# Score and maximum products of an attention layer, each split over the four 32-column tiles of TensorE

## The chip, the cores and the metric

The kernel runs on one core of one Trainium2 chip. The metric is the device time of the whole program in microseconds. A core has a matrix engine (TensorE, PE in the profile, with its weight loads shown apart as PEld), a vector engine (DVE), an activation engine (ACT), a general engine (POOL) and a queue engine (SP) that issues most of the transfers. PE writes to PSUM, which has eight banks of 128 partitions by 512 float32 here divided into three pools.

## The reference, cut to what matters

Two layers of the same shape, each an attention block and a small routed feed-forward block; only the attention matters here. S = 2048 tokens, D = 512, H = 32 query heads of 16 columns each, one key and one value head for all of them.

```python
q = (x @ wq).reshape(B, S, H, Dh)            # 32 heads of 16
k = x @ wk                                   # one key head
v = x @ wv                                   # one value head
scores = einsum("bhqd,bkd->bhqk", q, k) * (Dh ** -0.5)
p = softmax(scores, axis=-1)
o = einsum("bhqk,bkd->bhqd", p, v)
x = x + o.reshape(B, S, H * Dh) @ wo
```

Everything is float32 in and out.

## The kernel before, in words

**Units and steps.** A layer has 32 units (`u`), each of four heads by 512 query tokens, and a unit has 16 steps (`t`), so `layer` runs 512 steps. Each step makes four *scores* (128 keys by 512 columns of queries) and four *maximum products* (128 queries by 512 keys).

**Two products of the same operands.** `max_mm` multiplies 128 query columns by 512 keys into a bank of the pool psM (tile `pM`, four banks), and `nc.vector.reduce_max` (line 431) takes the row maximum of the bank into `mx`. This runs ahead of the scores by up to 12 steps. `scores` multiplies 128 keys by 512 query columns into a bank of the pool psS (tile `pS`, three banks), with the negated maximum in two extra rows, and ACT takes the exponential from PSUM (line 483) into `pr`. Both products are float16 and hold 48 or 50 rows of contraction: the operands `q_st` and `k_st` stand at partitions 0 to 49 and at 64 to 113, for two different pairs of heads. `h` picks the half; `max_mm` takes half `1 - n % 2` where the score beside it takes half `i % 2`, so a score and the maximum product next to it stand on different halves of the rows.

**The float32 products.** `pv_mm` multiplies `pr` by the values into the bank `pO` (line 510). It is issued as four products of 128 rows by 32 columns, one for each group of 32 PSUM partitions. `by_columns` (lines 184 to 188) does the same for the projections that `between` fits into free parts of that bank, and for others. A float32 product stands in the trace as two rows.

**What sets the order.** The program is in the order in which Python calls it (`manual_schedule`): per step `scores`, `max_mm` four times in turn, and after every third score (`RUN` = 3) a batch of `pv_mm` and one `between` piece. Below, a *score phase* is the three scores and three maximum products between two such batches, an *O phase* is the batch of 128-row products between two score phases, and a *round* is one of each. Other steps (projections, normalization, stores) are hung on steps by number.

Of the kernel before, what the change touches and what calls it, by code (L numbers as in the profile page):

```python
# [17 lines left out]
P = 128  # L18
# [6 lines left out]
CW = S // NCH  # L25
# [30 lines left out]
def interleaved_layers(ctx, tc, x_in, wq, wkv, wo, w_r, w_gate, w_up, w_down, out):  # L56
    nc = tc.nc
# [126 lines left out]
    def by_columns(out, lhsT, rhs, start, stop, shared=False):  # L184

        for j in range(4):
            r = slice(32 * j, 32 * (j + 1))
            nc.tensor.matmul(out[r], lhsT[:, r], rhs, start=start, stop=stop, skip_group_check=shared)  # L188
# [16 lines left out]
    def bank():  # L205
        pm = psM.tile([P, CW], F32, name="pM")
        return pm
# [102 lines left out]
    q_st, parts, pqs = {}, {}, {}  # L310
# [76 lines left out]
    def layer(li, src_d, dst_d, early=None):  # L387
        xld = xl_d[li]
        k_st, v_ext = k_sts[li], v_exts[li]
# [26 lines left out]
        def max_mm(mi, n):  # L416
            u, i = divmod(mi, 16)
            if i == 0 and n == 0:
                mx[u] = work.tile([P, 4, 16], F32, name="mx", bufs=3)
            pm = bank()  # L420
            nq = cuts[u]

            b, r = divmod(i, 16 // nq)
            x, c = divmod(r, 2)
            j, s = divmod(x, 4 // nq)
            h, c = 1 - n % 2, 2 * c + n // 2
            q = (b * 4 // nq + s) * P
            r = slice(h * HR, h * HR + KQ)
            nc.tensor.matmul(pm, q_st[u][r, j, q:q + P], k_st[r, c * CW:(c + 1) * CW], start=True, stop=True)  # L429
            i = b * 16 // nq + h * 8 // nq + 2 * s + j  # L430
            nc.vector.reduce_max(mx[u][:, c, i:i + 1], pm, axis=AX.X)  # L431

# [32 lines left out]
        def scores(t, i):  # L465

            u, r = divmod(t, KT)
            nq = cuts[u]
            b, r = divmod(r, KT // nq)
            w = CW // nq  # L470
            nk = nq // 2

            ps = bank() if mi == 16 * NU and i % 2 else psS.tile([P, CW], F32, name="pS")
            i, h = divmod(i, 2)
            hs = 2 * t + i
            if h == 0:
                pr[hs] = work.tile([P, 2, CW], F32, name="pr", bufs=6)
            rows = slice(h * HR, h * HR + KM)
            for k in range(nk):
                kt = r * nq + i * nk + k  # L480
                nc.tensor.matmul(ps[:, k * 2 * w:(k + 1) * 2 * w], k_st[rows, kt * P:(kt + 1) * P],  # L481
                                 q_st[u][rows, :, b * w:(b + 1) * w], start=True, stop=True)
            nc.scalar.activation(pr[hs][:, h, :], ps, AF.Exp, scale=DH ** -0.5)  # L483

        def pv_mm(hs, halves):
# [313 lines left out]
        for p in range(NCH * NG):  # L799
            e = 32 * p  # L800
            if p + 1 < NCH * NG:
                for n in range(4):
                    w = slice(n * P, (n + 1) * P)
# [10 lines left out]
            c, g = divmod(p - 1, NG)  # L814
            u = 2 * p - 1
# [7 lines left out]
        for c in range(NCH):  # L823
# [13 lines left out]
            for n, (t, kind) in enumerate(when):  # L837
                i = c * TPC + n // 4
                w = slice(n % 4 * OW, (n % 4 + 1) * OW)
# [98 lines left out]
        w = slice(2 * P, CW)  # L938
# [22 lines left out]
        for t in range(-LEAD0, last):  # L961
            tiles = []
            while mi < 16 * NU and made(mi) <= t:
                tiles.append(mi)
                mi += 1
            mms = [(m, n) for m in tiles for n in range(4)]
            mms = [first[4 * m + n] if 4 * m + n < len(first) else (m, n) for m, n in mms]
            for i in range(4):
                if t >= 0:
                    scores(t, i)  # L970
                for m, n in mms[len(mms) * i // 4:len(mms) * (i + 1) // 4]:
                    max_mm(m, n)
                if i == 3:
                    held.append(t)
                n = 4 * t + i
                if t < 0 or n % RUN == RUN - 1:

                    done = False
                    left = (n - RUN + 1) // 2 * 2 - ready
                    left = min(left, HALVES + (left > HALVES + 1))  # L980
                    while left > 0 and not done:
                        halves = range(ready % 2, 2) if left > 1 else range(ready % 2, ready % 2 + 1)
                        done = pv_mm(ready // 2, halves)
                        ready += len(halves)
                        left -= len(halves)
                    if ready and not done:
                        between(*at_block[0])
                    while held:
                        run(held.pop(0))
# [76 lines left out]
        for k in range(NDC):  # L1066
            for j in range(4):
                nc.tensor.matmul(gate[32 * j:32 * (j + 1), :FC], xsT[:, k, :], wgate_sb[:, k, j * FC:(j + 1) * FC],
                                 start=k == 0, stop=k == NDC - 1)
# [81 lines left out]
        for h in range(2):  # L1151
            w = slice(h * dh, (h + 1) * dh)
            for k in range(4):
                for j in range(4):
                    nc.tensor.matmul(pd[h][32 * j:32 * j + 2, :dh], hT[:, k, j, :], wd[4 * j + k][:, w],
                                     start=k == 0, stop=k == 3)
# [3 lines left out]
        for h in range(2):  # L1160
            w = slice(h * dh, (h + 1) * dh)
# [25 lines left out]
        for k in range(NDC):  # L1187
            if k % 2 == 0:
                w = slice(k * P, (k + 2) * P)
# [16 lines left out]
        w = slice(0, P)  # L1206
# [5 lines left out]
        for h in range(2):  # L1212
            r = slice(h * HR, h * HR + KQ)
# [5 lines left out]
        w = slice(P, 2 * P)  # L1219
# [38 lines left out]
    w = slice(0, 2 * P)  # L1258
# [61 lines left out]
```

## Time and profile before

| | |
|---|---|
| median of 2 runs | 2690.03 us (2689.11 to 2690.96) |
| the profiled execution | 2689.6 us |
| its span, first to last instruction | 2687.5 us |
| mean granted clock of TensorE | 0.986 of 2.4 GHz |
| PE, DVE, ACT busy | 2634.3, 2573.5, 2280.4 us |

Busy time of PE is the time in which at least one product is in the array by the trace's modelled ends. Products overlap, so its share doesn't say how much room PE has. That of DVE and ACT is the time in which an instruction of theirs runs.

### The profile page before, as it was taken

The numbers are of one execution on the slowest core, as the hardware profiler recorded it, in microseconds if no ns is written. First come the engines' busy times: TensorE is split into PE (matmuls) and PEld (weight loads), VectorE is DVE, ScalarE is ACT, GpSimd is POOL, SyncE is SP. The second block draws the span as 40 slices with busy tenths as digits, with TensorE's granted clock in tenths as the row PEclk, the third lists the DMA queues.
The fourth block names the chain that finished last, engine by engine and source line by source line (L and its number), as shares of the span: only waits on it lengthen the run. The fifth ranks groups of instructions, "written<-read, shape, count | busy, mean of one in ns | idle before, by whom it ended". The sixth has DMA issues, their size and how long they took to land.

```text
span 2687.5 us, 94488 instructions
## 1 busy us (share of the span) xinstructions
PE 2634.3 (98%) x39780; PEld 1238.4 (46%) x39780; DVE 2573.5 (96%) x4499; ACT 2280.4 (85%) x4710; POOL 770.1 (29%) x2039
## 2 busy tenths in 40 slices
PE   7999999999999999999999999999999999999999
PEld 3544444444444444444555444444444444444445
DVE  8999999999999999999669999999999999999995
ACT  2888888988889898889718888889898898988895
POOL 2100001122462126625521010021224522164262
PEclk8999999999999999999969999999999999999999
DMA  3001110000110001011400000000001100010114
GB/s 99 6 26 29 32 58 11 13 12 15 38 38 15 11 13 47 29 31 35 140 15 6 15 15 13 29 11 15 9 15 38 39 12 11 23 36 27 31 49 131
DMA packets 70764, 83.11 MB, mean 31 GB/s; under 512 B 27740, under 2 KB 43676, under 8 KB 70340
## 3 DMA queue, kind: packets, MB, share of 16 engines
q1 hardware_dynamic: 67474, 75.80, 9.2%
q8 instruction: 313, 5.13, 0.8%
q10 hardware_dynamic: 2354, 1.07, 0.1%
q14 instruction: 111, 0.91, 0.1%
q0 software_dynamic: 512, 0.20, 0.0%
HBM read 42.80 MB, written 17.18 MB: 22 GB/s over the span
## 4 chain that ended last, share of the span: by engine, by line
PE 78%; ACT 10%; DVE 5%; DMA 2%; issue 2%; POOL 2%; SPq 1%; ACTq 0%; DVEq 0%; POOLq 0%
PE pO L510 33%; PE pS L481 23%; PE pM L429 11%; ACT pr L483 8%; PE pO L188 5%; DVE mx L431 5%; PE pS L188 2%; DMA q_st<-mr 1%; SPq L460 1%; PE pM L454 1%; ACT so L516 1%; ACT qf L640 1%; DMA x<-xl_d,of 1%; ACT xT L259 0%; PE pS L258 0%
## 5 line engine op out<-in xcount | busy, mean ns | idle before, releaser
L431 DVE TENSOR_REDUCE mx<-pM 128x1 f32<-128x512 f32 x4096 | 2474.2, 683 | 30.6 <-PE pM L429 28.2
L483 ACT ACTIVATE pr<-pS 128x512 f32<-128x512 f32 x4044 | 2124.7, 605 | 237.4 <-PE pM L429 199.5
L429 PE MATMUL pM<-k_st,q_st 48*128 48x512 f16 x4096 | 1224.4, 385 | 8.8 <-DVE mx L431 5.8
L481 PE MATMUL pS<-q_st,k_st 50*128 50x512 f16 (+1 forms) x4248 | 1168.5, 371 | 17.4 <-DMA q_st<-mr 3.5
L510 PE MATMUL pO<-pr,v_ext 128*32 128x128 f32 (+1 forms) x22528 | 1174.9, 328 | 5.4 <-ACT so L516 3.2
L510 PEld LDWEIGHTS pO<-pr,v_ext 128*32 128x32 f32 x22528 | 562.3, 109 | 666.3 <-issue 453.5
L481 PEld LDWEIGHTS <-k_st 50*128 50x128 f16 x4352 | 298.2, 95 | 495.5 <-issue 350.6
L429 PEld LDWEIGHTS <-q_st 48*128 48x128 f16 x4096 | 288.7, 94 | 131.7 <-issue 101.9
L445 POOL TENSOR_SCALAR ma<-ma 128x8 f32<-128x8 f32 (+1 forms) x136 | 32.2, 237 | 809.1 <-DVE ma L439 809.1
L641 POOL TENSOR_TENSOR x<-x,qf 128x128 f32<-128x128 f32 x128 | 58.1, 455 | 493.6 <-ACT qf L640 493.5
L188 PE MATMUL pO<-xT,wq_sb 128*32 128x128 f32 x3584 | 180.0, 273 | 0.0
L346 POOL CAST qh<-qf 128x128 f16<-128x128 f32 x120 | 34.8, 290 | 444.2 <-ACT qf L345 434.6
L188 PE MATMUL pO<-wo_sb,so 128*32 128x128 f32 x2816 | 137.0, 273 | 0.0
L188 PEld LDWEIGHTS pO<-xT,wq_sb 128*32 128x32 f32 x3584 | 111.3, 110 | 34.0
L662 POOL TENSOR_TENSOR xh<-xh 128x128 f32<-128x128 f32 (+7 forms) x384 | 97.9, 255 | 30.1
L188 PEld LDWEIGHTS pO<-wo_sb,so 128*32 128x32 f32 x2816 | 86.6, 110 | 24.0
L724 POOL TENSOR_TENSOR xh<-xh 128x256 f32<-128x256 f32 (+8 forms) x216 | 66.4, 308 | 15.0
L516 ACT COPY so<-pO 128x256 f32<-128x256 f32 (+1 forms) x136 | 52.6, 387 | 2.1 <-PE pO L510 2.1
L456 ACT CAST mr<-pM 16x128 f16<-16x128 f32 (+1 forms) x136 | 34.6, 254 | 23.3 <-PE pM L454 14.6
L347 POOL TENSOR_TENSOR ql<-qf,qh 128x128 f16<-128x128 f32 x120 | 51.4, 428 | 9.7
L708 POOL TENSOR_SCALAR xh<-x,mv,rs 128x512 f32<-128x512 f32 x24 | 50.0, 2083 | 0.0
L188 PE MATMUL pS<-wo_sb,so 128*32 128x128 f32 (+1 forms) x896 | 41.9, 319 | 0.0
(260 smaller groups left out, 986.0 us busy)
## 6 DMA issues: line engine op xcount, KB each, us to landing
q_st<-mr SPq DMA_DIRECT2D x512, 1.0 KB
q_st<-qh SPq DMA_DIRECT2D x244, 32.0 KB
zt<-zr_d SPq DMA_DIRECT2D x120, 64.0 KB
xl_d<-xh SPq DMA_DIRECT2D x28, 256.0 KB
pr<-in_w_up SPq DMA_DIRECT2D x12, 448.0 KB
x<-in_x SPq DMA_DIRECT2D x20, 256.0 KB
x_d<-x SPq DMA_DIRECT2D x16, 256.0 KB
x<-x_d SPq DMA_DIRECT2D x16, 256.0 KB
```

The lines of the kernel that those rows point to most:

```text
L188: nc.tensor.matmul(out[r], lhsT[:, r], rhs, start=start, stop=stop, skip_group_check=shared)
L347: nc.gpsimd.tensor_tensor(ql, qf, qh, op=OP.subtract)
L429: nc.tensor.matmul(pm, q_st[u][r, j, q:q + P], k_st[r, c * CW:(c + 1) * CW], start=True, stop=True)
L431: nc.vector.reduce_max(mx[u][:, c, i:i + 1], pm, axis=AX.X)
L481: nc.tensor.matmul(ps[:, k * 2 * w:(k + 1) * 2 * w], k_st[rows, kt * P:(kt + 1) * P], q_st[u][rows, :, b * w:(b + 1) * w], start=True, sto ...
L483: nc.scalar.activation(pr[hs][:, h, :], ps, AF.Exp, scale=DH ** -0.5)
L510: nc.tensor.matmul(po[u][32 * j:32 * (j + 1), b * w + q.start:b * w + q.stop], v_ext[:, kt, 1 - u % 2:33 - u % 2], p[:, j % 2, k, j // 2, ...
L516: nc.scalar.copy(so[u][:, b * w:(b + 1) * w], po[u][:, b * w:(b + 1) * w])
L641: nc.gpsimd.tensor_tensor(x1[i][:, w], x1[i][:, w], y, op=OP.add)
L662: g.tensor_tensor(t[:, :n], t[:, :n], t[:, n:2 * n], op=OP.add)
L708: eng.tensor_scalar(xl, x1[i], mv2[m][:, b, 0:1], rs2[m][:, b:b + 1], op0=OP.subtract, op1=OP.mult)
L724: nc.gpsimd.tensor_tensor(rp_t[i][:, :n], rp_t[i][:, :n], rp_t[i][:, n:2 * n], op=OP.add)
```

## The change

Both float16 products go through `by_columns`, which the kernel already has: one product of 64 rows by 128 columns becomes four of 64 rows by 32 columns, each with its own weight load, on the column tiles j = 0 to 3, and each writes 32 partitions of the same bank. The moving operand, 512 elements long (256 where a unit is cut in four), is the same for the four. Nothing else is changed.

```diff
--- before.py
+++ after.py
@@ max_mm @@
             r = slice(h * HR, h * HR + KQ)
-            nc.tensor.matmul(pm, q_st[u][r, j, q:q + P], k_st[r, c * CW:(c + 1) * CW], start=True, stop=True)
+            by_columns(pm, q_st[u][r, j, q:q + P], k_st[r, c * CW:(c + 1) * CW], True, True)
             i = b * 16 // nq + h * 8 // nq + 2 * s + j
             nc.vector.reduce_max(mx[u][:, c, i:i + 1], pm, axis=AX.X)
@@ scores @@
-                nc.tensor.matmul(ps[:, k * 2 * w:(k + 1) * 2 * w], k_st[rows, kt * P:(kt + 1) * P],
-                                 q_st[u][rows, :, b * w:(b + 1) * w], start=True, stop=True)
+                by_columns(ps[:, k * 2 * w:(k + 1) * 2 * w], k_st[rows, kt * P:(kt + 1) * P],
+                           q_st[u][rows, :, b * w:(b + 1) * w], True, True)
```

PE's queue in the first layer before the change, the end of an O phase and the first two scores and maxima of the score phase behind it. What a product waits for stands in brackets, `Activation` for a free bank of psS and `DVE` for one of psM.

```order
L510 MATMUL pO<-pr,v_ext_117 32x128 x4
L188 MATMUL pO<-xT,wq_sb 32x128 x4
L481 LDWEIGHTS k_st
L481 MATMUL pS<-q_st,k_st 128x512 [waits Activation_49]
L429 LDWEIGHTS q_st
L429 MATMUL pM<-k_st,q_st 128x512 [waits DVE_49]
L481 LDWEIGHTS k_st
L481 MATMUL pS<-q_st,k_st 128x512 [waits Activation_49]
L429 LDWEIGHTS q_st
L429 MATMUL pM<-k_st,q_st 128x512 [waits DVE_49]
```

PE's queue after the change, the last of the four products of a score, the four of the maximum product next to it, and the O phase behind them. The two float16 products now carry the line of the helper, 188.

```order
L188 LDWEIGHTS k_st
L188 MATMUL pS<-q_st,k_st 32x512
L188 LDWEIGHTS q_st
L188 MATMUL pM<-k_st,q_st 32x512 [waits DVE_49]
L188 LDWEIGHTS q_st
L188 MATMUL pM<-k_st,q_st 32x512
L188 LDWEIGHTS q_st
L188 MATMUL pM<-k_st,q_st 32x512
L188 LDWEIGHTS q_st
L188 MATMUL pM<-k_st,q_st 32x512
L510 MATMUL pO<-pr,v_ext_117 32x256 x4
L510 MATMUL pO<-pr,v_ext_117 32x128 x4
```

A score phase thus grows from 6 loads and 6 products to 24 and 24, in the same order of scores and maxima, with each wait on the first of its four products. The queues of the other engines stand as before.

## Rows read from the trace of the kernel before

**Rows 1.** The page: the span, the engines' busy time, DVE's busy tenths in 40 slices, and the chain that ended last.

```profile
span 2687.5 us, 94488 instructions
...
PE 2634.3 (98%) x39780; PEld 1238.4 (46%) x39780; DVE 2573.5 (96%) x4499; ACT 2280.4 (85%) x4710; POOL 770.1 (29%) x2039
...
DVE  8999999999999999999669999999999999999995
...
PE 78%; ACT 10%; DVE 5%; DMA 2%; issue 2%; POOL 2%; SPq 1%; ACTq 0%; DVEq 0%; POOLq 0%
```

**Rows 2.** Groups of instructions by line and shape over the whole span: busy us, mean ns of one, idle time of the engine before them and what ended it.

```profile
L431 DVE TENSOR_REDUCE mx<-pM 128x1 f32<-128x512 f32 x4096 | 2474.2, 683 | 30.6 <-PE pM L429 28.2
L483 ACT ACTIVATE pr<-pS 128x512 f32<-128x512 f32 x4044 | 2124.7, 605 | 237.4 <-PE pM L429 199.5 <-PE pS L481 16.6 <-PE pM L481 8.5
L429 PE MATMUL pM<-k_st,q_st 48*128 48x512 f16 x4096 | 1224.4, 385 | 8.8 <-DVE mx L431 5.8 <-DMA q_st<-qh 1.6 <-ACT mr L456 0.5
...
L510 PEld LDWEIGHTS pO<-pr,v_ext 128*32 128x32 f32 x22528 | 562.3, 109 | 666.3 <-issue 453.5 <-ACT so L516 50.8 <-ACT qf L345 19.3
L481 PEld LDWEIGHTS <-k_st 50*128 50x128 f16 x4352 | 298.2, 95 | 495.5 <-issue 350.6 <-DMA q_st<-mr 5.0
```

**Rows 3.** The waits of DVE from 60 to 2640 us, longest first: who waited for whom, us in total, times, longest us.

```profile
DVE mx L431 <- PE pM L429: 26.7, 63, 1.6
DVE qf L607 <- PE pM L600: 7.3, 4, 3.6
```

**Rows 4.** PE's timeline (start us, us, instruction, count) around two rounds near 1080 us, where PE has no pause, and before them one long stretch of 128x32 products. Rows of the same kind that follow each other are merged, the length reaching to the end of the last.

```profile
1076.87 1.06 PE L188 MATMUL pS<-wo_sb,so 128*32 128x128 f32 x32
...
1079.69 0.28 PE L454 MATMUL pM<-ident,mp 128*16 128x128 f32 x1
1079.90 0.39 PE L481 MATMUL pS<-q_st,k_st 50*128 50x512 f16 x1
1079.90 0.60 PE L429 MATMUL pM<-k_st,q_st 48*128 48x512 f16 x2
1080.13 0.59 PE L481 MATMUL pS<-q_st,k_st 50*128 50x512 f16 x2
1080.35 0.38 PE L429 MATMUL pM<-k_st,q_st 48*128 48x512 f16 x1
1080.66 0.86 PE L510 MATMUL pO<-pr,v_ext 128*32 128x256 f32 x16
1081.33 0.40 PE L188 MATMUL pO<-wo_sb,so 128*32 128x128 f32 x8
1081.66 0.39 PE L481 MATMUL pS<-q_st,k_st 50*128 50x512 f16 x1
```

**Rows 5.** The same view near 703 us, a score phase in which PE waits, and the two reductions of DVE before it.

```profile
702.52 0.39 PE L481 MATMUL pS<-q_st,k_st 50*128 50x512 f16 x1
702.53 0.39 PE L429 MATMUL pM<-k_st,q_st 48*128 48x512 f16 x1
702.75 0.38 PE L481 MATMUL pS<-q_st,k_st 50*128 50x512 f16 x1
703.02 0.40 PE L429 MATMUL pM<-k_st,q_st 48*128 48x512 f16 x2
703.23 0.38 PE L481 MATMUL pS<-q_st,k_st 50*128 50x512 f16 x1
703.54 0.86 PE L510 MATMUL pO<-pr,v_ext 128*32 128x256 f32 x16
...
701.68 1.28 DVE L431 TENSOR_REDUCE mx<-pM 128x1 f32<-128x512 f32 x2
```

**Rows 6.** PE's groups by line and shape from 2100 to 2400 us.

```profile
L429 PE MATMUL pM<-k_st,q_st 48*128 48x512 f16 x492 | 144.6, 381 | 0.0
L481 PE MATMUL pS<-q_st,k_st 50*128 50x512 f16 x492 | 140.5, 380 | 1.9 <-DMA q_st<-mr 0.4
L510 PE MATMUL pO<-pr,v_ext 128*32 128x256 f32 x1312 | 101.9, 385 | 0.4
L510 PE MATMUL pO<-pr,v_ext 128*32 128x128 f32 x1312 | 67.9, 279 | 0.0
L188 PE MATMUL pO<-xT,wq_sb 128*32 128x128 f32 x488 | 24.5, 273 | 0.0
L188 PE MATMUL pO<-wo_sb,so 128*32 128x128 f32 x428 | 20.8, 273 | 0.0
L454 PE MATMUL pM<-ident,mp 128*16 128x128 f32 x16 | 4.4, 277 | 0.0
L188 PE MATMUL pS<-wo_sb,so 128*32 128x128 f32 x64 | 2.1, 274 | 0.0
```

**Rows 7.** Busy us (and instructions) of PE, PEld, DVE, ACT and POOL in three stretches, then the granted clock, the DMA share and GB/s.

```profile
701.52:701.55 0.03, 0.03 (x6) 0.02 (x4) 0.03 (x1) 0.03 (x1) 0.03 (x1) 1.00 0.00 0
...
2100.00:2400.00 300.00, 297.68 (x4604) 136.54 (x4604) 298.21 (x512) 268.98 (x554) 95.90 (x249) 1.00 0.07 22
78.00:98.00 20.00, 20.00 (x475) 14.39 (x475) 19.36 (x35) 16.71 (x36) 3.64 (x14) 1.00 0.01 3
```

**Rows 8.** The weight loads near the end of the program (line 1127), where products of 46 rows by 2 columns are followed by ones of 128 rows by 2 columns.

```profile
2678.89 0.08 PEld L1127 LDWEIGHTS pM<-token,hot 46*2 46x2 f32 x2
...
2679.01 0.11 PEld L1127 LDWEIGHTS pM<-token,hot 128*2 128x2 f32 x3
```

## The prediction

> **What bounds the kernel now.** The page comes first [rows 1]. PE is busy 98% of the span and its own chain blames PE for 78%, but both rest on modelled ends of products that overlap; neither says that PE is short of time. DVE is busy 2573.5 of 2687.5 us, and its tenths are nines except at the change of layer and the ends. The groups say with what [rows 2]: 4096 reductions of a maximum bank take 2474.2 us, 604 ns of DVE each, and in all of them DVE idled 30.6 us. In a stretch of full stream, 2100 to 2400 us, DVE is busy 298.2 of 300 us [rows 7]. The reductions are the bound, and the change touches none of them. Their part in PE's hands is the wait for a maximum product, 26.7 us in 63 places between 60 and 2640 us [rows 3]; the rest of DVE's idle time lies in the layer change, the start and the tail, which hold next to no score products. So a faster PE can give at most some 27 us, 1.0%. What a slower PE costs depends on its room.
>
> That room is seen in two timelines. Near 1080 us PE has no pause [rows 4]: score and maximum product start together at 1079.90, the second pair 0.23 us later, the third at 1080.35, the O phase at 1080.66. A pair takes 0.22 us as one product would, so the two halves of the rows run at the same time, and the unhindered score phase takes 0.76 us. In the second pair the maximum product stands in the record no later than the score that precedes it in the queue, so PE lets a row half that is free go first. Near 703 us [rows 5] the second maximum product waits until 703.02, just behind the reduction that ended at 701.68 + 1.28 = 702.96: its bank was not free. That score phase takes 1.02 us, because PE waits for DVE.
>
> Round by round, from 2100 to 2400 us [rows 6]: 492 scores are 164 rounds of 1.829 us. The groups of four 128x32 products take 0.109 us at 128 columns (eight groups in 1076.87 to 1077.93, seven steps and a last product of 0.27 to 0.28 us [rows 4]), and I take 0.218 at 256. There are 1312/4 = 328 groups of 256 and (1312 + 488 + 428 + 64)/4 = 573 of 128: 71.5 + 62.5 = 134 us, 0.82 us a round. The way back from the O phase costs 0.10 us on top (last group of 128 near 1081.44, next score 1081.66, 0.11 expected), the first group after a switch some 0.02, and the transposes (16 of 0.2 us in 164 rounds) 0.02. PE needs 0.76 + 0.82 + 0.14 = 1.72 us of 1.83 us. Its room is about **0.11 us a round**, with rounds of 16 products in the O phase far below and rounds of 24 (1.76 us from 1079.90 to 1081.66) close to the three reductions, 3 x 0.604 = 1.81 us.
>
> **The change, part by part.** All of it lies in the score phase, whose unhindered length I call 0.76 + X; the whole question is X against 0.11.
>
> *Issue.* A pair has eight loads and eight products instead of two and two. Between 701.52 and 701.55 four loads and four products of 128x32 start [rows 7]: 7 ns for a load and its product where the column tiles differ. Eight pairs of load and product are thus 0.055 us of issue in a pair's 0.22 us, and it doesn't add up from pair to pair, as groups of four follow each other at 0.109 us, the pace of one. What is left is skew: the maximum product's four start after the score's four, 4 x 7 = 28 ns later rather than 3, and the fourth column 3 x 7 = 21 ns behind the first. The last product of the phase starts about 0.045 us later, less what the pairs now lose to each other: **X = +0.035 us**.
>
> *Streaming.* Four moving streams of 64 rows in each half replace one. No row shows float16 on column tiles. The bounds are the pair in one pass (0.22 us, X as above) and no overlap of the halves or half-speed streams (0.44 us a pair, X = 0.66). I take the first: the 128x32 float32 products are four streams at once and lose nothing to each other [rows 4].
>
> *Switching.* From the last pair (1080.35) to the O phase (1080.66) pass 0.31 us, 0.09 more than a pair, and 0.10 on the way back. The new tile has the columns of the O phase's tile but not its rows. The nearest row is at the end of the program [rows 8]: the load of 128 rows by 2 columns starts 0.12 us after the pair of loads of 46 rows by 2 columns, where loads of one shape start within 0.03 us. So a change of rows alone still costs about 0.09, and I count no gain; the bounds are 0 and -0.19 us a round.
>
> *Weight loads.* They lie behind the running products but for the first after a switch; the row of the old load is 95 ns for 128 columns of float16, that of a 32-column load in float32 109 ns [rows 2]. At worst +0.015 us a round, inside the room. The Trainium skill speaks against the change here: TensorEngine Tiling (Array Packing), Restrictions and Gotchas, says that column tiling excludes Fast Weight Load. The two rows agree with it in so far as a quarter of the columns takes no less time; by it the sum would move by those 0.015 us at most, some 2 us in the end.
>
> *On the other engines* nothing changes. A maximum product's bank is full 0.05 us later; the four banks cover 4 x 0.6 = 2.4 us, so DVE doesn't see that. A score is ready as much later; ACT idles 237 us before its exponentials [rows 2].
>
> *The sum.* X = 0.035 leaves a mean room of 0.075 us. It costs where the room is already gone: behind the 63 waits of DVE. Counting two to three rounds for each (what four banks can bridge), 63 x 2.5 x 0.035 = 5.5 us. Against the profiled execution's 2689.6 us (0.4 below the median of 2690.03, which changes nothing) that gives **2695 us**. The skill's TensorE: Matmul & The Clock Gate, Measured speedup vs the span model, has about 4 ns for each further tile where this trace shows 7; by it X would be 0.02 and the sum 2693.
>
> **The rivals.**
>
> *A, a faster switch.* If the same column width spares the drain, the round loses 0.19 us and PE's waits on DVE grow instead. DVE's 26.7 us are all there is to win: about 2668 us. For it: both switches are visible gaps. Against it: rows 8. Chance 0.08.
>
> *B, strict order.* With 24 loads and 24 products in the phase PE may not look past a blocked row half as it does now. Then each pair waits for the one before in queue order, 28 ns at each of three and the skew: X about 0.09, mean room 0.02. The room spreads by some 0.11 to either side (O phases of 16 and of 24 products differ by 0.22 us), over three rounds some 0.06, so a mean shortfall of 0.015 us in 1365 rounds: +20 us, 2712 us. Chance 0.13.
>
> *C, the streams don't overlap* (slower). A score phase of six products in a row, 6 x 0.22 + 0.09 = 1.41 us, makes a round of 1.41 + 0.96 = 2.37 us against 1.83, which PE then sets: 0.54 x 1365 = 740 us, 3430 us at worst. It decides from X = 0.135: above that point each further 0.04 us of X is 55 us, 2%. For it: four float16 streams in each of two halves occur nowhere in the trace. Against: the float32 groups. Chance 0.09.
>
> *D, PE's queue can't feed it* (slower). A round now asks for 22 + 24 = 46 products with their loads in 1.83 us, 40 ns for each, through the whole stream, where 28 products stood before. The densest long stretch has 475 products and 475 loads in 20 us, 42 ns each [rows 7]. If that were the queue's own limit, a round would take 1.93 us: +140 us, 2830 us. Against it: in that stretch PE is kept by its array, as the groups there follow at the usual pace. Chance 0.07. The TensorE page (section Wait — 56ns, not 53.3ns?) names about 62 ns for a product where the sequencer decodes in software; by it 39,780 products [rows 1] and three more for each of the 4096 + 4352 split ones [rows 2], 65,124 in all, would take 4038 us, but 42 ns over 20 us lies below that, so this trace doesn't run that way.
>
> *E, it doesn't do what it says*, the four being issued one after another on one tile, is C's time.
>
> **How the numbers follow.** The forecast has 0.62 with 2687 to 2705 us around it, A 0.08, B 0.13, C 0.09, D 0.07; 0.01 is left. Two per cent (54 us, 2636 and 2744 us) is about what a measurement of this kernel can tell from no change. Forecast, A and B lie within: same 0.83 less a little of B's upper tail, 0.82. C and D are slower: 0.16. Faster would need more than DVE's idle time on PE: 0.02. The range runs from A's time to the point at which X = 0.13 would make PE the bound nearly everywhere: 2668 to 2738 us.
>
> **What the changed profile would show.** DVE's reductions unchanged at about 2474 us, with their wait on maximum products (now line 188) at 25 to 40 us. In a timeline of a phase without waits, six groups of four products, pairs 0.22 us apart, and the O phase 0.78 to 0.80 us after the first; if it is under 0.70, A; near 0.85, B; over 1.2, C. The load rows should keep near 100 ns. For D the groups would stand more than 40 ns a product apart with nothing waited for. The prediction is wrong if DVE shows long waits in the stream between 2100 and 2400 us, where it is busy 298.2 of 300 us now [rows 7].

## The result and the profile after

The changed kernel takes 2712.0 us (2709.7 to 2714.3, two runs) against 2690.0: ratio **1.0084**, 95% interval 1.0062 to 1.0106. Five further runs gave 2709.5 us and 1.0075 (1.0061 to 1.0089). It is slower, by some 20 us; the range of 2668 to 2738 held it, the forecast of 2695 was 17 us short. The profiled execution took 2714.3 us.

The page of the changed kernel, the rows that answer to [rows 1] and [rows 2]; scores and maximum products now carry line 188:

```profile
span 2712.2 us, 147092 instructions
...
PE 2660.5 (98%) x65124; PEld 1353.6 (50%) x65124; DVE 2579.2 (95%) x4499; ACT 2279.5 (84%) x4710; POOL 771.7 (28%) x2039
...
L431 DVE TENSOR_REDUCE mx<-pM 128x1 f32<-128x512 f32 x4096 | 2479.5, 682 | 47.6 <-PE pM L188 39.7
...
L188 PE MATMUL pM<-k_st,q_st 48*32 48x512 f16 x16384 | 1249.9, 387 | 7.2 <-DVE mx L431 4.6
...
L188 PEld LDWEIGHTS <-k_st 50*32 50x32 f16 x17408 | 403.4, 91 | 547.0 <-issue 427.7
```

Its waits of DVE from 60 to 2640 us, as in [rows 3], and its stretch from 2100 to 2400 us, as in [rows 7]:

```profile
DVE mx L431 <- PE pM L188: 37.8, 87, 1.7
```

```profile
2100.00:2400.00 300.00, 297.65 (x7464) 147.34 (x7459) 296.31 (x507) 266.79 (x548) 95.79 (x244) 1.00 0.08 23
```

Four products cost no more array time than one did: a maximum product takes 387 ns by the record (with modelled ends) where it took 385, and DVE's reduction is as long as before. What grew is DVE's idle time before it. PE's timeline of a round without waits, as in [rows 4]:

```profile
1083.00 0.40 PE L188 MATMUL pS<-q_st,k_st 50*32 50x512 f16 x4
1083.02 0.60 PE L188 MATMUL pM<-k_st,q_st 48*32 48x512 f16 x8
1083.24 0.59 PE L188 MATMUL pS<-q_st,k_st 50*32 50x512 f16 x8
1083.46 0.39 PE L188 MATMUL pM<-k_st,q_st 48*32 48x512 f16 x4
1083.78 0.86 PE L510 MATMUL pO<-pr,v_ext 128*32 128x128 f32 x16
```

The pairs stand 0.22 us apart, both row halves run together, and PE still takes the maximum product of the second pair ahead of the score (eight maximum products, then eight scores, in the order of the record). Over the 1320 phases of three scores and three maxima, the shortest twentieth of the score phases ends at 755 ns before and at 775 after: **X = 0.020 us**. The products start 3.3 ns apart, not 7, so the last one starts at 469 instead of 449 ns. In these phases the switch to the O phase stays (306 ns after the last start in both), and so does the one back (205 and 203).

Where the time went is seen by the start of DVE's n-th reduction in both traces (that of the further runs has a span of 2708.0 us). The changed kernel is 1.6 us late at the 576th and 10.9 at the 2047th; in the second layer 10.5 at the 2176th, 10.5 still at the 2624th, and 20.0 at the last. In the first part of each layer, from the 128th to the 576th and from the 2176th to the 2624th, it loses nothing: there no output projection stands in the O phases, and DVE's pitch is 598 ns from one reduction to the next in both kernels. All but some 1 us is lost where the output projection stands beside the attention, in 2943 reductions or 981 rounds, 0.019 us in each.

One more thing changed, which the diff doesn't show: ACT's queue. These are the instructions on the line of the exponential that do nothing but wait, before and after (count, ns min/median/max, first and last start):

```profile
L483 ACTq EVENT_SEMAPHORE  x118: 17/17/17, 50.2 to 2659.1; - x118
L483 ACTq EVENT_SEMAPHORE  x2034: 17/17/17, 51.2 to 2684.0; - x185
```

Half of the exponentials now have such an instruction ahead of them, and so two semaphore waits, one in each. Where ACT had been idle for over 0.2 us, an exponential without it starts 23 ns after the score's semaphore update, as before, and one with it 83 ns after: 60 ns later. Every kernel here with split scores has some 2000 of them; those with whole scores have 118.

### The profile page after: what moved, and what is told of

Its sections match the earlier page's. It is cut to its first block, busy times and chain, and to the rows that moved or that the text cites. A ratio compares the mean times of both kernels' runs of the same rounds, so it can differ in the third digit from the quotient of the medians.

```text
span 2712.2 us, 147092 instructions
## 1 busy us (share of the span) xinstructions
PE 2660.5 (98%) x65124; PEld 1353.6 (50%) x65124; DVE 2579.2 (95%) x4499; ACT 2279.5 (84%) x4710; POOL 771.7 (28%) x2039
## 3 DMA queue, kind: packets, MB, share of 16 engines
q10 hardware_dynamic: 2354, 1.07, 0.1%
## 4 chain that ended last, share of the span: by engine, by line
PE 79%; ACT 8%; DVE 3%; POOL 3%; issue 3%; DMA 2%; SPq 1%; ACTq 0%; DVEq 0%; POOLq 0%
PE pO L510 33%; PE pS L188 26%; PE pM L188 12%; ACT pr L483 7%; PE pO L188 5%; DVE mx L431 2%; SPq L460 1%; DMA q_st<-mr 1%; PE pM L454 1%; POOL xh L662 1%; ACT qf L640 0%; ACT xT L259 0%; PE pS L258 0%; DMA x<-xl_d,of 0%; PE pS L371 0%
## 5 line engine op out<-in xcount | busy, mean ns | idle before, releaser
L431 DVE TENSOR_REDUCE mx<-pM 128x1 f32<-128x512 f32 x4096 | 2479.5, 682 | 47.6 <-PE pM L188 39.7
L188 PE MATMUL pM<-k_st,q_st 48*32 48x512 f16 x16384 | 1249.9, 387 | 7.2 <-DVE mx L431 4.6
L188 PE MATMUL pS<-q_st,k_st 50*32 50x512 f16 (+1 forms) x16992 | 1201.7, 372 | 15.5 <-DMA q_st<-mr 4.1
L188 PEld LDWEIGHTS <-k_st 50*32 50x32 f16 x17408 | 403.4, 91 | 547.0 <-issue 427.7
L188 PEld LDWEIGHTS <-q_st 48*32 48x32 f16 x16384 | 370.8, 89 | 128.6 <-issue 103.6
L662 POOL TENSOR_TENSOR xh<-xh 128x128 f32<-128x128 f32 (+7 forms) x384 | 98.0, 255 | 30.1
```

What stands on the lines that cost most here:

```text
L662: g.tensor_tensor(t[:, :n], t[:, :n], t[:, n:2 * n], op=OP.add)
```

## The experiments

The first theory was: each round in which PE has no room pays X, and X is the later issue of the last product. Its rivals were a cost of the column tiles themselves, a cost that every round pays (queue, instruction fetch, PSUM), and the later arrival of results at ACT and DVE. The added waits on ACT were not among them, and no run was made for them.

**The changed kernel again.**

> The changed kernel once more, for a closer ratio. Theory (room): a score phase that nothing holds up has grown from 755 to 775 ns, and the time grows by up to 20 ns for each of the rounds in which PE has no room, so 2706 to 2716 us, ratio 1.006 to 1.010. Rival (chance of the runs): within 0.3% of before.

2709.5 us, 1.0075 (1.0061 to 1.0089). As expected; the cost is there.

**Two tiles of 64 columns** instead of four of 32.

```diff
+    def by_halves(out, lhsT, rhs):
+        for j in range(2):
+            r = slice(64 * j, 64 * (j + 1))
+            nc.tensor.matmul(out[r], lhsT[:, r], rhs, start=True, stop=True)
...
-            by_columns(pm, ..., True, True)
+            by_halves(pm, ...)
```

> Each score and maximum product as two products of 64 rows by 64 columns. Theory (issue skew): loads and products go out 3.3 ns apart per pair, a score phase has 12 of them in place of 24, the last of them starts about 7 ns later than before the change in place of 20, so X is 7 to 8 ns and the time 2690 + 22 x 7/20 = 2698 us, ratio 1.003. Rival (the cost comes with any column tile, whatever their number, for instance by slower weight loads): 2712 us like the changed kernel.

2708.4 us, 1.0072 (1.0058 to 1.0086): as slow as four tiles, so the issue alone isn't X. The first pair of a phase now lasts 240 ns where it lasted 226, and the last product starts at 470: X is 0.020 again, some 7 from issue and 14 from the first pair. The weight loads suggest why (by line and shape; the products of this kernel stand on line 194):

```profile
L194 PEld LDWEIGHTS <-k_st 50*64 50x64 f16 x8704 | 439.3, 105 | 537.7 <-issue 403.3 <-DMA q_st<-mr 3.6
```

A load of 64 columns takes 105 ns, one of 128 columns took 95 [rows 2] and one of 32 takes 91. After a switch the first load is not hidden (103 ns there, 92 before), and the first product of a phase is recorded at 400 ns instead of 387. The Trainium skill, TensorEngine Tiling (Array Packing), Restrictions and Gotchas, states that column tiling excludes Fast Weight Load. The trace agrees in so far as half the columns take 10 ns more; a quarter of the columns takes 4 ns less. By the second theory X has two parts, issue and an exposed first load. This kernel also has ACT's 2034 waits, so that it is as slow as four tiles fits them as well as an equal X.

**Only the maximum products split**, the scores whole.

```diff
-            nc.tensor.matmul(pm, q_st[u][r, j, q:q + P], k_st[r, c * CW:(c + 1) * CW], start=True, stop=True)
+            by_columns(pm, q_st[u][r, j, q:q + P], k_st[r, c * CW:(c + 1) * CW], True, True)
```

> Only the maximum products are split, the scores stay at 64 rows by 128 columns. Theory (the array drains whenever the tile shape changes, in columns too): score and maximum product no longer run at the same time and each change costs 0.09 us, so a score phase is 6 x 0.31 = 1.86 us, a round 2.8 us in place of 1.83, the time near 4000 us. Rival (row halves are independent, a change of columns alone costs nothing): X about 10 ns, the time near 2700 us.

5846 us, a single run. PE's timeline and a stretch of that kernel:

```profile
1501.32 0.60 PE L481 MATMUL pS<-q_st,k_st 50*128 50x512 f16 x1
1501.85 0.62 PE L188 MATMUL pM<-k_st,q_st 48*32 48x512 f16 x4
1502.40 0.60 PE L481 MATMUL pS<-q_st,k_st 50*128 50x512 f16 x1
1502.93 0.62 PE L188 MATMUL pM<-k_st,q_st 48*32 48x512 f16 x4
```

```profile
1000.00:1500.00 500.00, 500.00 (x3695) 151.56 (x3695) 208.53 (x310) 186.88 (x335) 36.98 (x109) 0.50 0.02 5
```

Scores and maxima, on different row halves, no longer overlap: 0.53 to 0.55 us from each to the next. A change of columns alone makes PE finish first, as the theory had it. The size was off because the granted clock was 0.50, the 1.2 GHz level, in this stretch, where in the kernel before it was 1.00 [rows 7]. From 870 to 960 us this kernel has a granted clock of 1.00, and there the steps are 0.31 to 0.33 us, as the theory had them:

```profile
901.26 0.39 PE L481 MATMUL pS<-q_st,k_st 50*128 50x512 f16 x1
901.57 0.40 PE L188 MATMUL pM<-k_st,q_st 48*32 48x512 f16 x4
901.90 0.39 PE L481 MATMUL pS<-q_st,k_st 50*128 50x512 f16 x1
...
870.00:960.00 90.00, 90.00 (x1171) 36.23 (x1167) 61.60 (x97) 57.49 (x106) 15.02 (x45) 1.00 0.02 6
```

**Three quarters of the output projection's products left out** beside the attention, without and with the split.

```diff
-        return [step(g) for g in gs], done
+        return [step(gs[0])], done
```

> The kernel before with three quarters of the output projection's products left out where they stand beside the attention (the pieces then sum one group of heads in place of all), which gives PE room: some 530 groups of 0.109 us less. Theory (room): DVE's pitch of 598 ns was exceeded by 29.6 us in all, nearly all of it where these pieces stand; most of that goes, so 2665 to 2675 us.

2668.5 us, as expected.

> The changed kernel with the same products left out. Theory (room): with room in PE the longer score phase is hidden, so 0 to 8 us above the run without the split and with the same products left out. Rival (a cost that every round pays, for instance PE's queue or the instruction fetch, or later banks for DVE): 20 to 25 us above it.

2677.0 us, 8.5 above it where the full kernels lie 20 apart. DVE's idle time before its reductions goes from 19.2 to 22.3 us, where the full kernels have 30.6 [rows 2] and 47.6:

```profile
L431 DVE TENSOR_REDUCE mx<-pM 128x1 f32<-128x512 f32 x4096 | 2467.5, 680 | 19.2 <-PE pM L429 17.5
L431 DVE TENSOR_REDUCE mx<-pM 128x1 f32<-128x512 f32 x4096 | 2470.0, 680 | 22.3 <-PE pM L188 18.7
```

So more than half of the cost is bound to the rounds that are full; a cost that every round pays in full is out. What remains is a little more than the theory's 0 to 8.

**The maximum over 256 of 512 keys**, without and with the split.

```diff
-            nc.vector.reduce_max(mx[u][:, c, i:i + 1], pm, axis=AX.X)
+            nc.vector.reduce_max(mx[u][:, c, i:i + 1], pm[:, :CW // 2], axis=AX.X)
```

> The kernel before with the maximum taken over 256 of each 512 keys (half of the keys are left out of the maximum), which takes DVE out of the way. Theory: PE is then the bound of the stream with 1.72 us a round (ACT has some 1.65): 1365 x 1.72 + 190 = 2540 us.

2618.8 us, not 2540. DVE is out of the way (its reductions take 1493 us), yet by the prediction's 190 us outside the stream a round takes (2619 - 190) / 1365 = 1.78 us. The timeline of PE and ACT shows why:

```profile
1562.47 3.12 ACT L483 ACTIVATE pr<-pS 128x512 f32<-128x512 f32 x6
...
1563.59 0.39 PE L481 MATMUL pS<-q_st,k_st 50*128 50x512 f16 x1
1563.59 0.60 PE L429 MATMUL pM<-k_st,q_st 48*128 48x512 f16 x2
1563.82 0.65 PE L481 MATMUL pS<-q_st,k_st 50*128 50x512 f16 x2
1564.10 0.39 PE L429 MATMUL pM<-k_st,q_st 48*128 48x512 f16 x1
1564.41 0.86 PE L510 MATMUL pO<-pr,v_ext 128*32 128x256 f32 x16
```

ACT runs six exponentials without a pause; the third score of the phase starts at 1564.09 (its row of two ends at 1564.47, a product is 0.38 long) and not at 1564.04, and the phase lasts 0.82 us. The score phases of this kernel have a mean of 832 ns against an unhindered 755, though hardly a maximum product waits for DVE: PE also waits for ACT's three banks.

> The changed kernel with the maximum over half of the keys. Theory (the split lengthens each score phase by 20 ns, and nothing hides it when PE is the bound): 1365 x 0.020 = 27 us above the unsplit kernel with the same reduction. Rival (the split costs DVE, which finds its banks later or slower): no more than 5 us above it. Rival (ACT takes over as the bound): under 15 us above it.

2648.9 us, 30.1 above it: 0.022 us a round. With DVE out of the way about the whole X is paid; ACT's added waits are in this pair too, so the two aren't told apart. (The maximum over half the keys is also the fastest kernel here, but the exponentials then lack a bound that holds for any input, so it is no version of the same computation.)

**RUN = 4**, without and with the split: four scores to a phase, a quarter fewer switches.

```diff
-RUN = 3
-HALVES = 3
+RUN = 4
+HALVES = 4
```

> The kernel before with RUN = 4 and HALVES = 4: a batch of 128-row products after every fourth score instead of every third, so a quarter fewer changes of tile shape. Theory (room): each change there and back costs 0.19 us, so PE gains 0.19/3 - 0.19/4 = 0.016 us a score, 0.047 us in what three scores take, and the places where DVE now waits for a maximum product lose most of their 30 us: 2665 to 2680 us. Rival (the four banks of maxima are too few for a longer O phase, 1.1 to 1.5 us): DVE waits in each round, 2700 us or more.

2896.6 us. Neither theory nor rival: the fourth score waits for the first exponential of its own phase, since psS has three banks. Timeline of the unsplit kernel:

```profile
1601.77 0.39 PE L481 MATMUL pS<-q_st,k_st 50*128 50x512 f16 x1
...
1602.19 2.06 ACT L483 ACTIVATE pr<-pS 128x512 f32<-128x512 f32 x4 [0.33 <-PE pM L429]
...
1602.84 0.37 PE L481 MATMUL pS<-q_st,k_st 50*128 50x512 f16 x1 [0.24 <-ACT pr L483]
```

> The changed kernel with RUN = 4 and HALVES = 4. Theory (room): the split adds 20 ns to a score phase of now four scores, 15 ns in what three scores take, and PE has 47 ns more room there, so it lies 5 to 12 us above the unsplit kernel with RUN = 4 and below the unsplit kernel with RUN = 3, 2672 to 2688 us. Rival (a cost that every product pays): 20 us or more above the unsplit kernel with RUN = 4.

2989.1 us, 92.5 above it, 0.09 us for each of its 1024 rounds. The same places of the split kernel:

```profile
1602.92 0.40 PE L188 MATMUL pS<-q_st,k_st 50*32 50x512 f16 x4
...
1603.43 2.06 ACT L483 ACTIVATE pr<-pS 128x512 f32<-128x512 f32 x4 [0.46 <-PE pM L188]
...
1604.08 0.40 PE L188 MATMUL pS<-q_st,k_st 50*32 50x512 f16 x4 [0.31 <-ACT pr L483]
```

The exponential starts 0.51 us after the score's start where it started 0.42 after it, and the fourth score follows 1.16 after the first instead of 1.07. So a split score's exponential starts later, and where PE waits for ACT in every round all of that is paid. The delay has two parts. Over the exponentials that ACT began after an idle time of more than 0.2 us, those without a wait instruction ahead of them start 423 ns after the start of the score in the unsplit kernels and 448 in the changed one; those with it start 508 ns after it. With RUN = 4 nearly all of these exponentials have it (710 of 724), so the delay is 85 ns, near the 0.09 us that each round pays. With RUN = 3 it is about half (254 of 526): 25 ns for the others and 85 for these, 50 in the mean. The reductions that DVE waited for (idle for more than 50 ns) start 455 ns after the start of the maximum product before and 494 after (medians).

**The last maximum product in two parts**, 172 + 340 and 76 + 436 keys, without column tiles.

```diff
+            for x, y in ((0, 172), (172, CW)) if turn["cut"] else ((0, CW),):
+                nc.tensor.matmul(pm[:, x:y], q_st[u][r, j, q:q + P], k_st[r, c * CW + x:c * CW + y], start=True, stop=True)
...
+                    turn["cut"] = t >= 0 and (4 * t + i) % RUN == RUN - 1
                     max_mm(m, n)
```

> The kernel before, unsplit, with only the last maximum product of each score phase issued as two products along its 512 keys, 172 and 340. The first takes 72 ns, less than the weight load of the second (92 ns, which can start only when the first does), so the score phase grows by about 20 ns, as the change's does, with no column tile and no skew. Theory (the time follows the length of the score phase alone): about 20 us above before, 2705 to 2715 us. Rival (the loss comes from the results of split products reaching ACT and DVE 26 and 40 ns later, not from PE's length): under 8 us above before.

2691.7 us, 1.0004 (0.9995 to 1.0014).

> The same with 76 and 436 keys: the first takes 32 ns, so the score phase grows by about 60 ns. Theory (length alone, in four rounds of five): 1365 x 0.8 x 0.060 = 65 us above before, 2740 to 2765 us. The working of the prediction (cost only behind DVE's waits, mean room 0.11 us a round): about 63 x 2.5 x 0.060 = 10 us above before.

2692.8 us, 1.0011 (1.0001 to 1.0020). Neither decides what it was to decide: the second part started 77 and 37 ns after the first, without a load between them, and the phase grew by 5 ns in both (760 for 755).

**A further product of 40 columns** ahead of the last maximum product, with the same weights.

```diff
-            for x, y in ((0, 172), (172, CW)) if turn["cut"] else ((0, CW),):
+            for x, y in ((0, 40), (0, CW)) if turn["cut"] else ((0, CW),):
```

> The kernel before, unsplit, with a further product of 40 columns ahead of the last maximum product of each score phase (its columns are written again by the full product). The two cuts of that product lengthened the phase by 5 ns only, since the second part of the same weights started 77 and 37 ns after the first; a repeat of 40 columns adds its own 17 to 25 ns and those 5, so X is 20 to 30 ns, as much as the change's 20 or a little more, and no result of a split product comes later. Theory (the time follows the length of the score phase): 20 to 30 us above before, 2710 to 2720 us. Rival (most of the loss is that split products reach ACT and DVE 26 and 40 ns later): by the cuts' slope, 1.4 to 2.6 us for 5 ns, 6 to 12 us above before, 2696 to 2702 us.

2700.8 us, 1.0039 (1.0026 to 1.0053), so 11.4 us for a score phase of 780 ns: X = 0.025, no split and no added wait on ACT (118 such instructions, as before); the last maximum product of each phase comes 29 ns later, which is in the 11.4 us. Its trace loses the time in the same places, 5.8 us between the 576th and the 2047th reduction and 5.6 from the 2624th on. By this slope the change's X of 0.020 costs 9 us (6 to 11 by the interval); the change costs some 20. The theory of length alone falls: it accounts for about half.

A rough count over the traces says where the other half may lie. In the phases of three scores and three maxima, take by how much a score or a maximum product starts later than in an unhindered phase, and put it down to the semaphore update just before it. PE waited for DVE's reductions some 85 us in the kernel before, 72 with the repeat and 65 in the changed kernel; for ACT's exponentials 61, 59 and 74. A longer phase takes up waiting on both; the split adds waiting on ACT.

## Why the prediction was right, and where its steps failed

**What bounds the kernel** held: DVE's reductions didn't get longer, no gain came, and the loss is small. That the 98% of PE says nothing held too: it is 98% still.

The signs that it named came out: DVE's wait on maximum products is 37.8 us, the O phase follows 0.78 us after the first product, and DVE is busy 296.31 of 300 us in the stream.

**Issue**: the mechanism was right and the size too large. X was put at 0.035 with 7 ns for a load and its product, a spacing read from float32 products; the float16 ones start 3.3 ns apart, and X is 0.020. The Trainium skill's about 4 ns for each further tile (TensorE: Matmul & The Clock Gate, Measured speedup vs the span model) is nearer to this trace.

**Streaming, switching, order** came out as forecast. Four float16 streams in each row half run at the pace of one, the two switches cost what they did, and the record's order shows that B's mechanism isn't there. B's 2712 us, the measured time, is a coincidence: its X of 0.09 isn't in the trace, and its own sum, 2690 and 20, is 2710. (A's time is a slip too: 2689.6 less 26.7 is 2663, not 2668.)

**Weight loads**: right for 32 columns, 91 ns against the 109 taken as the worst. Loads got longer only with 64 columns, 105 ns, a case that the prediction didn't treat.

**The sum** is the step that failed. It counted 63 waits times 2.5 rounds, 5.5 us for X = 0.035, by which 0.020 would have cost 3 us; measured is 9 us for such an X alone (the repeat of 40 columns), three times as much. Under it lies the room of 0.11 us a round. It took all of PE's waiting for waiting on DVE, after the one phase in [rows 5]; by the count above PE waits some 61 us for ACT beside the 85 for DVE. With DVE out of the way a round still takes 1.78 us, 0.05 less than before and not 0.11: the rest is in the main PE waiting for ACT's banks. And a mean over a stretch hides that the rounds with projection products sit together; where none are, the loss is zero.

**"On the other engines nothing changes"** failed, and with it "A score is ready as much later; ACT idles" and "DVE doesn't see that". The queues of the other engines do not stand as before: 1916 exponentials have got a wait instruction of their own. Where ACT is idle, exponentials start 25 ns later, and 85 ns later with that instruction; maxima reach DVE some 40 ns later, and DVE waits 87 instead of 63 times. About half of the loss isn't explained by PE's length. That it is these delays, those of the exponentials above all, is the likely reading: PE's waiting for ACT grows by some 13 us, and the kernel with four scores a phase shows the delay being paid in full. No run here took the delays alone away, or the added waits alone, so it is inferred from a remainder and a count, and not shown.

**Luck.** An X that was too large and a cost of it that was too small partly made up for each other, and the half of the loss that the prediction put at nothing still left the time inside a range whose upper end came from another case, X = 0.13.

## What to carry to other kernels

Room has to be measured against everything that an engine waits for: take the bounding engine's work down in one run and see which time remains. Here the average of demand over a stretch gave twice the room that there was. Splitting a product over column tiles that overlap anyway added no array time, but the last tile started later and the result came later; the first cost about half of the loss, and the second is the likely other half. Compare the queues of all engines as built, not only the diff: a split on PE put waits into ACT's queue. And if one product of an interleaved pair is split, the other has to have the same tiles: with one split alone this kernel took more than twice the time.

## What the runs showed of the hardware

A product on a tile of other columns ended the overlap of two row halves, even though its rows were free: 0.31 to 0.33 us from one product to the next at the 2.4 GHz level, where a pair took 0.22 us, and 0.53 to 0.55 us at 1.2 GHz. With that alternation the granted clock was 0.50 from 1000 to 1500 us, though the record has PE busy for 500 of the 500 us. A weight load of float16 took 95 ns for 128 columns, 105 for 64 and 91 for 32. Float16 products on different column tiles started 3.3 ns apart, float32 ones 7 ns. An exponential behind a wait instruction of its own started 83 ns after the semaphore update, one that waits itself 23 ns after it. PE keeps up with 65,124 products and as many loads in 2712 us, and with 7464 products in 300 us, 40 ns each, more than its queue had been seen to carry for long before.
